# Logarithms of both parities of w in two steps, an earlier output of step 7, and halved dummy matmuls in an attention-then-MoE kernel

## The chip, the cores and the metric

The kernel runs on one core of a Trainium2 chip. The metric is the device time of one execution in microseconds (us), lower is better; where several executions were timed, the median is given. A core has five engines with a queue each: TensorE (PE in the profile, its weight loads PEld), VectorE (DVE), ScalarE (ACT), GpSimd (POOL) and SyncE (SP, which here issues all DMAs). Each engine does its instructions in the order of its queue, and waits on semaphores for the others.

## The reference

A recurrence over 768 positions (4 batches, 8 heads, 48 channels a head), whose output goes through two matrices with a squared ReLU between them:

```python
for t in range(S):
    cur = einsum('bhd,bhe->bhde', u[None] * k[t], v[t])
    y[t] = einsum('bhd,bhde->bhe', r[t], state + cur)
    state = w[t][:, :, :, None] * state + einsum('bhd,bhe->bhde', k[t], v[t])
x = y.transpose(0, 2, 1, 3).reshape(3072, 384)
out = maximum(x @ w_in, 0) ** 2 @ w_out        # w_in 384 x 2048, w_out 2048 x 384
```

All inputs and the output are float32; the values of w lie between 0.8 and 0.95.

## The kernel before

The 3072 tokens are done in 12 steps of 256. A tile has 128 partitions, and partition p holds two successive tokens, the *parities* j = 0 and 1. So `raw["w", s]` is `[128, 8 heads, 2 parities, 48]`.

**The attention half of a step** turns the recurrence into matmuls over chunks of 128 tokens. `ww_` multiplies the w of both parities (line 272), `lw_` takes the logarithm of the product on ScalarE (276) into `lw_buf`, and `cum_` sums the logarithms along the chunk with two triangular matrices, `tri_strict` and `tri_incl_neg`, and for each half chunk with `half_ones` (332 to 336) into a PSUM tile `att`. `exp_` (348) makes the decays of it in place, and `ac_` (354) those of a whole half chunk. `rd_.s.0` and `rd_.s.1` (366, 369) multiply r and k with the decays on VectorE. In the first steps TensorE transposes them (`tr_`, 382) and `rkt_` copies the results to SBUF (396), in later steps a DMA does (`dtr_`). `p_` (422, 425) multiplies the two, `pm_` (438, 441) masks the result, `su_` (453) makes the change of the state, `ts_` and `sn_` (463, 468) the next state, `y_` and `yc_` (490, 502) the output. The part with u goes beside this: `ku_` (305) multiplies k by u, `qp_` (310) by r, `q_` (315) sums over the channels, `qs_` and `vs_` (285) rearrange rows, `vq_` (324) multiplies. `ysb_` (513) adds it to the output into `y_sb`, and `yt_` with `xt_` (525, 530), or a DMA `dyt_` (534), transposes that to `xT`. `rw_` and `kw_` (294, 298) multiply r and k of one parity with w beforehand, `v_` (280) casts v.

**The MoE half of a step** is `m1_.s.g` (545, six 256-wide matmuls, g from 0 to 7), `rl_` (ReLU), `sq_` (square), `m2_` (576), `os_` and `store`.

**Order.** The scheduler is off. The string `ORDER` holds words, and each engine's queue is the order of its own words there. A word is an operation, the step and further numbers; `=V`, `=A`, `=G` name the engine where there is a choice (VectorE, ScalarE, GpSimd), and `:0` to `:3`, `:m`, `:b` the PSUM bank or banks. `ld.` words are loads on SP. Attention of steps 0 to 2 fills the opening; then the MoE half of a step and the attention of later steps share TensorE.

**Dummies.** `warm_.n.i.x` (596) puts n matmuls of 512 columns into bank i whose result nobody reads. They are in TensorE's queue like any other work, and stand only ahead of the first MoE matmul, `m1_.0.3`. There are 51 of them.

Of the kernel before, what the change touches and what calls it, by code (L numbers as in the profile page):

```python
# [16 lines left out]
ORDER = """  # L17
ld.0.w ld.0.k ld.0.u ld.0.r ld.1.w ww_.0=V lw_.0 warm_.11.5.0 cum_.0:0 ub_.0:2 kw_.0=G exp_.0 uc_.0=A warm_.4.5.1
rd_.0.1 ld.0.v tr_.0.1:0 rkt_.0.1=A ld.1.k ld.1.r rw_.0=G ld.2.w ku_.0=G rd_.0.0 ld.1.v warm_.3.5.2 tr_.0.0:1 ww_.1=V
rkt_.0.0=A qp_.0=V ld.2.r v_.0=A warm_.5.5.3 p_.0.0:m p_.0.1:1 ac_.0 lw_.1 q_.0 su_.0:b ld.2.k cum_.1:0 ts_.0.0=A  # L20
kw_.1=G pm_.0.0 pm_.0.1 vs_.0.0=A sn_.0.0 ld.1.i exp_.1 rw_.1=G vs_.0.1=A qs_.0=A warm_.3.2.4 ku_.1=G rd_.1.0 rd_.1.1
warm_.2.2.5 ts_.0.1=V qp_.1=V warm_.7.2.6 ld.0.i tr_.1.0:0 rkt_.1.0=V warm_.2.3.21 tr_.1.1:2 ac_.1 sn_.0.1 q_.1
ww_.2=G rkt_.1.1=A vs_.1.0=A lw_.2 v_.1=G y_.0:0 yc_.0.1 warm_.2.3.22 p_.1.1:1 p_.1.0:m warm_.6.1.7 vq_.0=G pm_.1.1
cum_.2:1 vs_.1.1=A pm_.1.0 qs_.1=A exp_.2 warm_.4.1.8 su_.1:m kw_.2=G ysb_.0=V rw_.2=G ts_.1.0=V warm_.1.0.23 y_.1:0
rd_.2.1 yc_.1.0 rd_.2.0 yt_.0:1 xt_.0=V sn_.1.0 cast.i.1=A vq_.1=G ts_.1.1=V warm_.1.0.24 tr_.2.1:2 yc_.1.1 ld.2.v
tr_.2.0:0 m1_.0.3:1 rkt_.2.1=A m1_.0.2:2 ac_.2 ysb_.1=V yt_.1:3 rkt_.2.0=A sn_.1.1 p_.2.1:1 rl_.0.3=A cast.i.0=V
p_.2.0:0 xt_.1=A ku_.2=V m1_.0.1:0 vs_.2.1=G m1_.1.0:3 m1_.1.2:1 vs_.2.0=A rl_.0.1=A m1_.1.1:0 v_.2=G rl_.0.2=A
rl_.1.0=A rl_.1.2=A qp_.2=G pm_.2.1 pm_.2.0 su_.2:1 rl_.1.1=V ts_.2.0=V ld.2.i m1_.0.0:2 m1_.1.3:1 cast.i.2=A y_.2:1
q_.2 yc_.2.0 sn_.2.0 yc_.2.1 rl_.1.3=A m1_.0.5:3 ld.3.i m1_.1.5:1 ld.3.w m1_.0.4:0 rl_.0.0=A rl_.0.5=V qs_.2=A
rl_.1.5=A cast.i.3=G m1_.1.7:3 ld.0.o m1_.1.4:1 vq_.2=V ysb_.2=V rl_.0.4=A rl_.1.7=A ww_.3=G cast.o.0=G m1_.0.7:2  # L30
yt_.2:3 ld.2.o m1_.0.6:0 lw_.3 cast.o.2=G cum_.3:1 xt_.2=V rl_.0.7=V ld.3.o m1_.2.4:3 rl_.0.6=V sq_.0.1=A ld.1.o
sq_.0.0=A rl_.1.4=A m1_.2.2:2 sq_.0.2=A m1_.1.6:0 m1_.2.7:1 ld.3.r rl_.1.6=A sq_.1.1=A rl_.2.2=V rl_.2.4=V m1_.2.5:2
# [617 lines left out]
```

## Time and profile before

| | |
|---|---|
| time, median of 3 runs | 178.65 us (178.42 to 179.02) |
| the profiled execution | 178.38 us |
| its span, first to last instruction | 176.6 us |
| TensorE busy | 171.2 us, 97% of the span |
| VectorE busy | 138.4 us, 78% |
| ScalarE busy | 134.0 us, 76% |
| GpSimd busy | 110.0 us, 62% |

A row of the timeline gives start, duration, engine, line, operation, output<-inputs, shapes and a count; in brackets stands how long the engine was idle before and who released it. Two rows from the beginning of GpSimd's timeline, the last of its memsets and its first product:

```profile
3.12 0.53 POOL L248 MEMSET lw_buf<- 128x512 bf16 x1
6.19 1.00 POOL L298 TENSOR_TENSOR k_raw<-k_raw,w_raw 128x384 f32<-128x384 f32 x1 [2.55 <-DMA k_raw<-in_k_dram]
```

The chain of waits that ended last lies on TensorE for 91% of the span; most of it is the MoE matmuls of lines 545 and 576, and 3.7% are dummies of line 596.

### The profile page before, as it was taken

The page shows a single profiled execution, that of the slowest core. Times are in us where ns is not written, and L with a number is a line of the kernel's source. Part 1 is how long each engine was busy: PE and PEld are TensorE (multiplying, and loading weights), DVE is VectorE, ACT ScalarE, POOL GpSimd, SP SyncE. Part 2 cuts the span into 40 slices and gives each one's busy share as a digit, 9 for nine tenths or more (in the row PEclk, how much of TensorE's full clock was granted, in tenths as well). Part 3 has the DMA queues.
Part 4 walks back from the last instruction along what each step waited for, and adds up shares of the span by engine and source line. Part 5 has one row for each costly group of instructions (what it writes and reads, how often), then busy time and mean ns, then how long its engine had stood idle before and what let it go on. Part 6 is the DMA issues. An engine that isn't in the chain of part 4 may idle for free.

```text
span 176.6 us, 5525 instructions
## 1 busy us (share of the span) xinstructions
PE 171.2 (97%) x2296; PEld 124.7 (71%) x2296; DVE 138.4 (78%) x205; ACT 134.0 (76%) x240; POOL 110.0 (62%) x132
## 2 busy tenths in 40 slices
PE   7889999999999999999999999999999999999993
PEld 2355488887766777678677777688776778768763
DVE  5499999779997998998988989976779693804430
ACT  5497999999899659899889979779976428863501
POOL 6558999860796147998599788979997803000000
PEclk9999999999999999999999999999999999999999
DMA  5999999999999599999999999997956710622203
GB/s 140 262 261 265 304 352 344 366 346 253 262 261 284 123 147 234 183 282 256 276 266 159 234 234 234 186 198 163 298 138 126 105 29 17 106 59 89 89 4 134
DMA packets 78954, 35.61 MB, mean 202 GB/s; under 512 B 72145, under 2 KB 77394, under 8 KB 78930
## 3 DMA queue, kind: packets, MB, share of 16 engines
q1 hardware_dynamic: 78930, 35.27, 89.2%
q8 instruction: 18, 0.29, 0.7%
q14 instruction: 6, 0.05, 0.1%
HBM read 25.17 MB, written 4.72 MB: 169 GB/s over the span
## 4 chain that ended last, share of the span: by engine, by line
PE 91%; DVE 3%; DMA 2%; ACT 1%; issue 1%; DVEq 0%; ACTq 0%
PE m L545 19%; PE m L576 18%; PE bk L576 18%; PE bk L545 17%; PE att L490 3%; DMA w_raw<-in_w_dram 2%; PE m L596 2%; PE att L502 2%; PE att L453 2%; PE att L425 2%; PE bk L596 2%; DVE ww L272 1%; PE att L334 1%; PE bk L382 1%; PE att L332 1%
## 5 line engine op out<-in xcount | busy, mean ns | idle before, releaser
L545 PEld LDWEIGHTS <-wi_sb 128*128 128x128 bf16 x576 | 54.8, 98 | 10.0 <-DMA xT<-y_sb 0.2
L576 PEld LDWEIGHTS <-gt 128*128 128x128 bf16 x400 | 37.7, 98 | 19.5 <-ACT gt L562 0.2
L545 PE MATMUL m<-xT,wi_sb 128*128 128x256 bf16 x300 | 39.4, 273 | 0.0
L562 ACT ACTIVATE gt<-gt 128x1024 bf16<-128x1024 f16 x37 | 38.2, 1052 | 0.5
L545 PE MATMUL bk<-xT,wi_sb 128*128 128x256 bf16 x276 | 36.5, 273 | 0.0
L576 PE MATMUL bk<-wo_sb,gt 128*128 128x384 bf16 (+2 forms) x208 | 36.0, 314 | 0.0
L576 PE MATMUL m<-wo_sb,gt 128*128 128x384 bf16 x192 | 35.0, 326 | 0.0
L554 ACT ACTIVATE gt<-m 128x512 f16<-128x512 f32 x32 | 18.8, 595 | 11.0 <-PE m L545 10.6
L554 ACT ACTIVATE gt<-bk 128x512 f16<-128x512 f32 x36 | 21.0, 596 | 7.6 <-PE bk L545 7.4
L556 DVE TENSOR_SCALAR gt<-m 128x512 f16<-128x512 f32 x18 | 12.3, 687 | 13.0 <-PE m L545 12.6
L441 DVE TENSOR_TENSOR pmT<-att,mask 128x1024 bf16<-128x1024 f32 x16 | 19.1, 1215 | 1.1 <-PE att L425 0.9
L324 POOL TENSOR_TENSOR ku<-v_sh,qs 128x768 f32<-128x768 bf16 x9 | 13.3, 1475 | 8.6 <-ACT qs L285 8.5
L468 POOL TENSOR_TENSOR S<-t_state,ac_buf 128x192 bf16<-128x192 f32 x20 | 11.9, 595 | 10.0 <-DVE t_state L463 9.0
L305 POOL TENSOR_TENSOR ku<-k_raw,u_bc 128x768 f32<-128x768 f32 x9 | 16.7, 1855 | 0.6 <-DMA k_raw<-in_k_dram 0.6
L298 POOL TENSOR_TENSOR k_raw<-k_raw,w_raw 128x384 f32<-128x384 f32 x8 | 8.0, 1005 | 9.9 <-DMA k_raw<-in_k_dram 9.9
L513 DVE TENSOR_TENSOR y_sb<-att,ku 128x768 bf16<-128x768 f32 x12 | 11.5, 954 | 3.5 <-PE att L490 1.5
L369 DVE TENSOR_TENSOR kdec_buf<-k_raw,att 128x768 bf16<-128x768 f32 x12 | 11.4, 947 | 3.1 <-ACT att L348 3.1
L285 ACT CAST v_sh<-v_raw 64x384 bf16<-64x384 f32 x26 | 13.2, 509 | 0.3
L310 POOL TENSOR_TENSOR ku<-ku,r_raw 128x768 f32<-128x768 f32 x7 | 12.7, 1809 | 0.2
L366 DVE TENSOR_TENSOR rdec_buf<-r_raw,att 128x384 bf16<-128x384 f32 x24 | 12.2, 544 | 0.4 <-POOL r_raw L294 0.4
L285 POOL CAST v_sh<-v_raw 64x384 bf16<-64x384 f32 x18 | 10.6, 589 | 1.4 <-DMA v_raw<-in_v_dram 0.5
L315 DVE TENSOR_REDUCE q<-ku 128x16 f32<-128x768 f32 x12 | 11.3, 944 | 0.1
(107 smaller groups left out, 255.0 us busy)
## 6 DMA issues: line engine op xcount, KB each, us to landing
w_raw<-in_w_dram SPq DMA_DIRECT2D x12, 384.0 KB, 5.6
k_raw<-in_k_dram SPq DMA_DIRECT2D x12, 384.0 KB, 6.4
r_raw<-in_r_dram SPq DMA_DIRECT2D x12, 384.0 KB, 5.7
v_raw<-in_v_dram SPq DMA_DIRECT2D x12, 384.0 KB, 6.2
out_dram<-o_sb SPq DMA_DIRECT2D x23, 192.0 KB, 3.3
w_st<-in_moe_w_in_dram SPq DMA_DIRECT2D x4, 768.0 KB, 8.9
w_st<-in_moe_w_out_dram SPq DMA_DIRECT2D x4, 768.0 KB, 7.3
kT<-kdec_buf SPq DMA_TRANSPOSE x8, 4.6
```

The source lines that it names most:

```text
L285: copy(out[j * Q:(j + 1) * Q, c], src[c * Q:(c + 1) * Q, :, j])
L305: tensor_mul("ku_", s, h)(tiles["ku", s][:, hs], raw["k", s][:, hs, 1:3, :], u_bc[:, hs, None, :].to_broadcast([C, n, 2, D]))
L310: tensor_mul("qp_", s, h)(ku, ku, raw["r", s][:, heads(h), 0:2, :])
L324: tensor_mul("vq_", s)(vq[:], tiles["vs", s][:], tiles["qs", s][:, :, :, None].to_broadcast([C, 2, H, D]))
L366: nc.vector.tensor_mul(rdec[0][:, ps, j, :, 0:D], x[:, :, j, :].rearrange("p (a e) d -> p a e d", e=2), dec.rearrange("p (a e) d -> p a e ...
L441: nc.vector.tensor_mul(pmT, ps_p[:].rearrange("p e (x t) -> p (e x) t", t=C), mk.to_broadcast([C, 8, C]))
L468: nc.gpsimd.tensor_mul(t[:], tiles.pop(("ts", s, c))[:].rearrange("p (a d) -> p a d", a=HP), tiles["a_c", s][:, :, c, None].to_broadcast([ ...
L545: nc.tensor.matmul(ps1[:, j, :], wi_sb[:, n // 4, kk, n % 4 * 128:(n % 4 + 1) * 128], tiles["xT", s][:, :, kk, :], start=(kk == 0), stop=( ...
L554: nc.scalar.activation(rl, m1, AF.Relu, scale=RS)
L556: nc.vector.tensor_scalar(out=rl, in0=m1, scalar1=RS, scalar2=0.0, op0=ALU.mult, op1=ALU.max)
L562: nc.scalar.activation(gt, rl, AF.Square)
L576: nc.tensor.matmul(m2, gt[:, 4 * q + n, rows * C:(rows + 1) * C], wo_sb[:, 4 * q + n, cols], start=(summed[s, c] == 1 and n == 0), stop=(s ...
```

## The change

1. In steps 1 and 2 the word `ww_` is gone: `lw_` takes the logarithm of both parities at once, straight from the loaded w, into a new tile `lw_pair`, which GpSimd clears at the start. `cum_` then does each of its sums as two accumulating matmuls, one a parity.
2. `ku_.0` goes from GpSimd to VectorE, `vs_.1.0` from ScalarE to GpSimd, `rl_.6.5` from VectorE to ScalarE.
3. Some words move: in step 0 and 1 `ac_.0`, `exp_.1`, `rd_.1.1`, `qs_.1` and `su_.1`; three dummies go ahead of `tr_.0.1`, four halves ahead of `p_.0`; `m1_.3.3` goes ahead of two `m2_`; in steps 7 and 8 `vq_.7` and `ysb_.7` go ahead of `q_.8`, `ld.10.w` ahead of two transposes on SP, and `kw_.8`, `pm_.7.1`, `qs_.8`, `ww_.10` change places.
4. Dummies whose last number is 6 or more become twice as many of 256 columns: 23 of the 51 become 46. Between `p_.1.0` and `cum_.2` now stand 14 halves, then 2 ahead of `su_.1` and 8 between `su_.1` and `y_.1`; before it was 6 wholes, then 4, then 1 there.

```diff
+    SHORT = 6
+    PAIR_LN = {int(w.split(".")[1]) for w in ORDER.split() if w.startswith("lw_.")} - {
+        int(w.partition("=")[0].split(".")[1]) for w in ORDER.split() if w.startswith("ww_.")}
+    lw_pair = consts.tile([C, 2, H, DP], BF16)
...
+        if PAIR_LN:
+            nc.gpsimd.memset(lw_pair[:], 0.0)
...
     def lw_(s, h=None):
+        if s in PAIR_LN:
+            nc.scalar.activation(lw_pair[:, :, :, 0:D].rearrange("p j h d -> p h j d"), raw["w", s][:], AF.Ln)
+            return
...
     def cum_(s, h=None):
-        lw, hs = lw_bufs[s % NLW], heads(h)
+        hs = heads(h)
...
+        logs = [lw_pair[:, j] for j in range(2)] if s in PAIR_LN else [lw_bufs[s % NLW][:]]
+        ends = dict(start=(True, False), stop=(False, True)) if s in PAIR_LN else dict(start=(True,), stop=(True,))
+        sums = [(cs[:, 0, 0:n], tri_strict)] + ([] if s in ONE_SUM else [(cs[:, 1, 0:n], tri_incl_neg)])
         for p in pairs(h):
-            nc.tensor.matmul(cs[:, 0, DM + 2 * p:DM + 2 * p + 2], lw[:, 2 * p:2 * p + 2, :],
-                             half_ones[:], start=True, stop=True)
-        nc.tensor.matmul(cs[:, 0, 0:n], tri_strict[:], lw[:, hs, 0:D], start=True, stop=True)
-        if s not in ONE_SUM:
-            nc.tensor.matmul(cs[:, 1, 0:n], tri_incl_neg[:], lw[:, hs, 0:D], start=True, stop=True)
+            for lw, start, stop in zip(logs, ends["start"], ends["stop"]):
+                nc.tensor.matmul(cs[:, 0, DM + 2 * p:DM + 2 * p + 2], lw[:, 2 * p:2 * p + 2, :],
+                                 half_ones[:], start=start, stop=stop)
+        for into, tri in sums:
+            for lw, start, stop in zip(logs, ends["start"], ends["stop"]):
+                nc.tensor.matmul(into, tri[:], lw[:, hs, 0:D], start=start, stop=stop)
...
     def warm_(n, i, x=0):
-        for _ in range(n):
-            nc.tensor.matmul(quad[i][:] if i < 4 else att[i - 4][:, 0, :], warm[:, 0:C], warm[:],
-                             start=True, stop=True)
+        bank = quad[i][:] if i < 4 else att[i - 4][:, 0, :]
+        m = 512 if x < SHORT else 256
+        for _ in range(n * 512 // m):
+            nc.tensor.matmul(bank[:, 0:m], warm[:, 0:C], warm[:, 0:m], start=True, stop=True)
...
-rkt_.0.0=A qp_.0=V ld.2.r v_.0=A warm_.5.5.3 p_.0.0:m p_.0.1:1 ac_.0 lw_.1 q_.0 su_.0:b ld.2.k cum_.1:0 ts_.0.0=A
+rkt_.0.0=A qp_.0=V ld.2.r v_.0=A warm_.2.3.21 warm_.5.5.3 p_.0.0:m p_.0.1:1 lw_.1 q_.0 su_.0:b ld.2.k cum_.1:0
```

How the queues stand at three places. VectorE, from the products of r in step 0 to those of step 1, before:

```order
L366 TENSOR_TENSOR rdec_buf_109<-r_raw,att_86 128x4x2x48 x2
L272 TENSOR_TENSOR ww<-w_raw 128x384
L310 TENSOR_TENSOR ku<-ku,r_raw 128x768
L315 TENSOR_REDUCE q<-ku 128x16
L438 TENSOR_TENSOR pmT<-m_0_90,mask 128x512
L438 TENSOR_TENSOR pmT<-m_1_91,mask 128x512
L441 TENSOR_TENSOR pmT<-att_87,mask 128x1024
L366 TENSOR_TENSOR rdec_buf_111<-r_raw,att_86 128x4x2x48 x2
L369 TENSOR_TENSOR kdec_buf_112<-k_raw,att_86 128x16x48
```

and with the change:

```order
L379 TENSOR_TENSOR rdec_buf_110<-r_raw,att_86 128x4x2x48 x2
L315 TENSOR_TENSOR ku<-k_raw,u_bc 128x768
L320 TENSOR_TENSOR ku<-ku,r_raw 128x768
L325 TENSOR_REDUCE q<-ku 128x16
L451 TENSOR_TENSOR pmT<-m_0_90,mask 128x512
L451 TENSOR_TENSOR pmT<-m_1_91,mask 128x512
L454 TENSOR_TENSOR pmT<-att_87,mask 128x1024
L382 TENSOR_TENSOR kdec_buf_113<-k_raw,att_86 128x16x48
L379 TENSOR_TENSOR rdec_buf_112<-r_raw,att_86 128x4x2x48 x2
```

`ww_.1` has given its place to `ku_.0`, and the products of k in step 1 (`kdec_buf`) now come ahead of those of r (`rdec_buf`). ScalarE, from the copies of step 0 to the exponential of step 1, before:

```order
L396 COPY kT<-bk_88 128x1024
L396 COPY rT<-bk_89 128x1024
L280 CAST v_bf<-v_raw 128x8x2x48
L354 ACTIVATE ac_buf_105<-att_86 128x8
L276 ACTIVATE lw_buf_104<-ww 128x8x48
L461 COPY t_state<-bk_88 128x192
L285 CAST v_sh<-v_raw 64x384 x2
L348 ACTIVATE att_86<-att_86 128x2x384
```

and with the change:

```order
L409 COPY kT<-bk_88 128x1024
L367 ACTIVATE ac_buf_106<-att_86 128x8
L409 COPY rT<-bk_89 128x1024
L290 CAST v_bf<-v_raw 128x8x2x48
L283 ACTIVATE lw_pair<-w_raw 128x8x2x48
L474 COPY t_state<-bk_88 128x192
L361 ACTIVATE att_86<-att_86 128x2x384
L295 CAST v_sh<-v_raw 64x384 x4
```

`ac_.0` has moved up between the copies, the logarithm is twice as large, and the exponential of step 1 no longer has two casts in front of it. GpSimd, in the stretch ahead of `vq_.0`, before:

```order
L305 TENSOR_TENSOR ku<-k_raw,u_bc 128x768
L468 TENSOR_TENSOR S<-t_state,ac_buf_105 128x192
L272 TENSOR_TENSOR ww<-w_raw 128x384
L280 CAST v_bf<-v_raw 128x8x2x48
L324 TENSOR_TENSOR ku<-v_sh,qs 128x768
```

and with the change:

```order
L315 TENSOR_TENSOR ku<-k_raw,u_bc 128x768
L481 TENSOR_TENSOR S<-t_state,ac_buf_106 128x192
L295 CAST v_sh<-v_raw 64x384 x2
L290 CAST v_bf<-v_raw 128x8x2x48
L334 TENSOR_TENSOR ku<-v_sh,qs 128x768
```

The two casts of `vs_.1.0` stand where `ww_.2` stood.

More of the change, by code (lines that the diff above doesn't have):

```diff
@@ L23 @@
[L23 to L32, printed above, removed]
@@ L89 @@
+store.11.2 os_.11.3=A store.11.3
 """
```

127 lines of the change are left out of this document (68 added, 59 removed).

## The prediction

> **What bounds the kernel now.** I read the page's first line, then the busy time by stretch, then the four engines' rows of the opening in order of time.
>
> ```profile
> span 176.6 us, 5525 instructions
> 13.00:25.00 12.00, 11.69 (x174) 7.01 (x174) 12.00 (x19) 10.29 (x23) 11.32 (x12) 1.00 1.13 297
> 25.00:174.00 149.00, 148.81 (x2025) 112.68 (x2022) 117.70 (x171) 115.58 (x204) 91.38 (x104) 1.00 0.88 195
> ```
>
> The columns are stretch, length, then the busy time of PE, PEld, DVE, ACT and POOL. From 25 us on TensorE has no gap to speak of (148.81 of 149.00), and no dummy is left there. Whatever the change does after 25 us can win at most those 0.19 us. So the time is set by when the first matmul of the MoE half, `m1_.0.3`, starts: before it TensorE is kept full with dummies, and VectorE has no pause either (12.00 of 12.00). What each waits for, VectorE first:
>
> ```profile
> 9.12 1.68 DVE L272 TENSOR_TENSOR ww<-w_raw 128x384 f32<-128x384 f32 x1
> 10.72 0.94 DVE L310 TENSOR_TENSOR ku<-ku,r_raw 128x768 f32<-128x768 f32 x1
> ...
> 14.90 1.01 DVE L366 TENSOR_TENSOR rdec_buf<-r_raw,att 128x384 bf16<-128x384 f32 x2
> 15.82 0.95 DVE L369 TENSOR_TENSOR kdec_buf<-k_raw,att 128x768 bf16<-128x768 f32 x1
> ...
> 19.28 1.21 DVE L441 TENSOR_TENSOR pmT<-att,mask 128x1024 bf16<-128x1024 f32 x1
> ...
> 21.61 0.95 DVE L513 TENSOR_TENSOR y_sb<-att,ku 128x768 bf16<-128x768 f32 x1
> ...
> 24.59 0.55 DVE L530 COPY xT<-bk 128x768 bf16<-128x768 bf16 x1
> ```
>
> The last of these rows, `xt_.0`, ends at 25.14, and `m1_.0.3` starts at 25.19: VectorE's full queue is what the MoE half now waits for. TensorE over the same time:
>
> ```profile
> 7.17 1.04 PE L596 MATMUL att<-warm 128*128 128x512 bf16 x4
> 8.33 0.62 PE L382 MATMUL bk<-ident,kdec_buf 128*128 128x128 bf16 x8
> ...
> 12.37 0.25 PE L332 MATMUL att<-half_ones,lw_buf 128*128 128x2 bf16 x4
> 12.48 0.32 PE L334 MATMUL att<-lw_buf,tri_strict 128*128 128x384 bf16 x1
> 12.64 0.32 PE L336 MATMUL att<-lw_buf,tri_incl_neg 128*128 128x384 bf16 x1
> 13.31 2.75 PE L596 MATMUL m<-warm 128*128 128x512 bf16 x12 [0.34 <-DVE pmT L438]
> 15.89 0.63 PE L382 MATMUL bk<-ident,rdec_buf 128*128 128x128 bf16 x8
> ...
> 16.83 0.62 PE L382 MATMUL m<-ident,kdec_buf 128*128 128x128 bf16 x8
> 18.56 0.40 PE L422 MATMUL att<-rT,kT 64*128 64x128 bf16 x8
> 19.12 1.47 PE L596 MATMUL bk<-warm 128*128 128x512 bf16 x6
> ...
> 21.93 0.44 PE L453 MATMUL m<-v_bf,kdec_buf 64*64 64x48 bf16 x32
> 22.30 0.39 PE L596 MATMUL bk<-warm 128*128 128x512 bf16 x1
> 22.61 0.56 PE L490 MATMUL att<-v_sh,pmT 128*128 128x48 bf16 x16
> 25.19 0.82 PE L545 MATMUL bk<-xT,wi_sb 128*128 128x256 bf16 x6
> 25.84 0.82 PE L545 MATMUL m<-xT,wi_sb 128*128 128x256 bf16 x6
> ```
>
> A row's duration holds the tail of its last matmul, so I count from start to start: 12 dummies from 13.31 to 15.89, 0.215 us each.
>
> **The change, part by part.** *VectorE loses `ww_.1` and gets `ku_.0`.* `ww_.1` took 1.68 us; it ran while GpSimd did `ku_.0` (first row below, to 10.39). The new `ku_.0` has 768 elements a lane of two SBUF tensors, as the 0.94 us row at 10.72 has; the group of its own shape is slower, mean 1.05.
>
> ```profile
> 8.58 1.81 POOL L305 TENSOR_TENSOR ku<-k_raw,u_bc 128x768 f32<-128x768 f32 x1
> 12.21 1.01 POOL L298 TENSOR_TENSOR k_raw<-k_raw,w_raw 128x384 f32<-128x384 f32 x1 [1.82 <-DMA k_raw<-in_k_dram]
> 18.24 1.00 POOL L272 TENSOR_TENSOR ww<-w_raw 128x384 f32<-128x384 f32 x1
> 19.96 1.48 POOL L324 TENSOR_TENSOR ku<-v_sh,qs 128x768 f32<-128x768 bf16 x1
> L285 POOL CAST v_sh<-v_raw x4: 500/684/1142, 26.1 to 46.1; 64x384 bf16<-64x384 f32 x4
> L305 DVE TENSOR_TENSOR ku<-k_raw,u_bc 128x768 f32<-128x768 f32 x3 | 3.1, 1049 | 0.0
> ```
>
> I take 0.95, since GpSimd is then empty until its 12.21 row, which waits for a DMA: VectorE gains 1.68 - 0.95 = 0.73 us (0.63 by the mean). It would be through `pm_.0.1` and ready for step 1's decay products at 14.90 - 0.73 = 14.17.
>
> *But those need `exp_.1`, and its chain on ScalarE and TensorE gets longer.*
>
> ```profile
> 8.98 1.01 ACT L396 COPY kT<-bk 128x1024 bf16<-128x1024 bf16 x1 [1.24 <-PE bk L382]
> 10.08 1.01 ACT L396 COPY rT<-bk 128x1024 bf16<-128x1024 bf16 x1
> 10.99 0.83 ACT L280 CAST v_bf<-v_raw 128x768 bf16<-128x768 f32 x1
> 11.72 0.18 ACT L354 ACTIVATE ac_buf<-att 128x8 f32<-128x8 f32 x1
> 11.79 0.52 ACT L276 ACTIVATE lw_buf<-ww 128x384 bf16<-128x384 f32 x1
> 13.52 0.79 ACT L348 ACTIVATE att<-att 128x768 f32<-128x768 f32 x1
> 17.48 1.01 ACT L396 COPY kT<-m 128x1024 bf16<-128x1024 bf16 x1 [0.44 <-PE m L382]
> ```
>
> 1. Three dummies now stand ahead of `tr_.0.1`: seven from 7.17 take 7 x 0.215 = 1.50, so it starts at 8.67, not 8.33.
> 2. On ScalarE `rkt_.0.1` moves from 8.98 to 9.32. A 1.01 us copy frees the engine after 0.91 (10.08 to 10.99); `ac_.0`, now behind it, after 0.07 (11.72 to 11.79). `rkt_.0.0` at 10.30, `v_.0` at 11.21, and after 0.73 (10.99 to 11.72) `lw_.1` at 11.94.
> 3. `lw_.1` has 768 elements instead of 384. The cast of 768 took 0.83, the exponential of 768 0.79: 0.83, with 0.52 and twice that as the far ends. It ends at 12.77 instead of 12.31.
> 4. `cum_.1` then runs 4 more two-column matmuls at (12.48 - 12.37)/4 = 0.03 and two more at 0.16 (12.48 to 12.64): +0.43 on the 0.59 from 12.37 to the end of the 12.64 row. From 12.83 to 13.85.
> 5. `exp_.1`, no longer behind two casts, runs 13.9 to 14.7, against 13.52 to 14.31. VectorE goes on at about 14.8, against 14.90.
>
> So 0.6 of the 0.73 us turns into a wait of VectorE. The ends of step 3 move this by -0.3 and +0.2.
>
> *The decay products change places.* Before, the products of r were ready at 15.91 and transposed while those of k were made; `tr_.1.1` began at 16.83. Now k comes first, but TensorE still transposes r first, and r is ready at 14.8 + 0.87 + 1.01 = 16.68. Then `tr_.1.0` goes at 16.74 and `tr_.1.1` 0.45 later (its 0.62 less the tail of 0.17 by which the 25.19 row outlasts the next start): 17.19, +0.36. `rkt_.1.1` goes from 17.48 to 17.84 and `p_.1.1` from 18.56 to 18.92. VectorE has its `pm_.1.1` ready for it at about the old 19.28, so it loses only 0.1 here.
>
> *TensorE from `p_.1.1` to `y_.1`.* Work, all in one queue: the p matmuls 0.56 (18.56 to 19.12), 14 half dummies, `cum_.2` 0.43 + 0.43 (12.37 to 12.64 and 0.16, and step 4), 2 halves, `su_.1` 0.37 (21.93 to 22.30), 8 halves. A half costs 0.109: the 25.19 and 25.84 rows are six 256-wide matmuls in 0.65, each with its weight load. That gives 0.56 + 1.53 + 0.86 + 0.22 + 0.37 + 0.87 = 4.41, and `y_.1` at 23.33 instead of 22.61. It was waiting for `y_sb`, which ended at 22.56; with VectorE 0.1 later that wait ends before the dummies do. From `y_.1` to `m1_.0.3` were 2.58 us. One dummy of 0.215 in them now stands further ahead, so at most 2.37 is left; some of that was waiting for VectorE, as `m1_.0.3` itself did, and I put it at 0.2, an estimate: 23.33 + 2.17 = 25.50. **`m1_.0.3` comes 0.3 us later**, bounded by VectorE's 0.1 below and by ScalarE above: its `rkt_.2` copies follow `tr_.2.1`, 0.4 late.
>
> *Steps with cover.* The clearing of `lw_pair` comes before GpSimd's first product, which waits for a DMA. The Ln of step 2 adds 0.3 us to ScalarE, which in the same place gives two casts of `vs_.1.0` away. Both at 0; without cover 0.3 for the Ln and 1.1 for the clearing, twice what the 0.53 us memset of half the size took.
>
> The price of a half dummy could be otherwise by one rule: the Trainium skill, "TensorE: Matmul & The Clock Gate", Back-to-back issue gap, gives a sustained stream of weight loads and matmuls about 131 ns per matmul at N=512 and 81 ns at N=128, by which two halves would cost more than a whole. Here the trace has 215 ns at 512 and 109 ns at 256, so it differs, and the rows stand; by the page the 46 halves would add at least 46 x 81 - 23 x 131 = 713 ns, an estimate.
>
> *Step 7.* `y_sb` of step 7 moves ahead of the reduction `q_.8`.
>
> ```profile
> 113.67 0.55 PEld L545 LDWEIGHTS <-wi_sb 128*128 128x128 bf16 x6 [0.25 <-DMA xT<-y_sb]
> 113.68 0.83 PE L545 MATMUL m<-xT,wi_sb 128*128 128x256 bf16 x6
> ```
>
> Its transposed copy is what the first weight load of `m1_.7.7` waited 0.25 us for. TensorE itself shows no gap, so I count 0 (to -0.2, the whole idle time above). `q_.8` and `qs_.8` come that much later; they feed `y_sb` of step 8, two steps of TensorE work on. `ld.10.w` passes the two transposes of step 7 in SP's queue, whose results `p_.7` takes; this, `m1_.3.3`, `kw_.8` and `rl_.6.5` on ScalarE lie where TensorE shows no wait: 0, and at most a few tenths if one of them makes a wait.
>
> **Sum.** The profiled execution took 178.38 us (span 176.6 and 1.8 around it): 178.38 + 0.3 = 178.68. The median of the three runs is 0.27 above that execution, so the forecast is 178.65 + 0.3 = **178.95**, itself between 178.5 and 179.4. About 0.3%, here 0.54 us, is what a measurement of this kernel can tell from no change.
>
> **Rivals.** *Faster: VectorE's gain goes through.* VectorE is the engine without a pause; if `exp_.1` ends by 14.1, so an `lw_.1` 0.6 us earlier than I work out, `p_.1.1` comes at 18.92 - 0.63 = 18.29. TensorE's 4.41 us then bring `y_.1` to 22.70 and `m1_.0.3` to 24.9, 0.3 early: 178.35. The whole 0.7 (177.95) would also need dummies shorter than their rows. For it: VectorE's full row. Against: steps 1 to 4, each from a row. Chance 0.18, of which I give a third to more than 0.54 us.
>
> *Slower: GpSimd becomes the bound of `y_sb`.* `ww_.2` (18.24, 1.00) is replaced by the two casts of `vs_.1.0`, at 0.50 to 1.14 each. At 1.14 each `vq_.0`, which ended at 21.44, ends at about 22.7; VectorE's `ysb_.0` starts 1.1 late, and everything behind it in VectorE's full queue to `xt_.0`: 178.65 + 1.1 = 179.75. At 0.50 each nothing changes; it decides from about 1.4 us for both. In that slot the three GpSimd rows of before show no slowing, so I hold it for the less likely end, 0.20. The Trainium skill, "GPSIMD Engine Reference", Specifications, says the SBUF interfaces are shared with VectorE, in contention with instructions of two SBUF inputs. The 1.68 us `ww_.1` beside GpSimd agrees; VectorE's work in the new slot has mostly a PSUM input, so the rule speaks for the low end.
>
> *Nothing in the opening moves the end*: the dummies only fill what is waited for, 178.65. Chance 0.10; the forecast has 0.52.
>
> **How the numbers follow.** Faster by over 0.54 us (under 178.11) is a third of the first rival, 0.06, and 0.06 for causes that I don't see: 0.12. Slower (over 179.19) is the second rival and the upper part of the forecast, 0.10: 0.30. The rest, 0.58, is within. The range runs from 178.1, which takes in the first rival's likely price, to 179.7, which takes in most of the second's.
>
> **What would show it.** Right: VectorE idle about 0.6 us before the products of k of step 1, released by `exp_.1`; `tr_.1.1` near 17.2; no TensorE wait between the 14 halves and `y_.1`; `m1_.0.3` near 25.5; the rest without gaps. Wrong: `exp_.1` ending before 14.2; `vq_.0` ending after 21.7; halves not at 0.109; or TensorE gaps after 26 us.

## The result and the profile after

| | before | changed |
|---|---|---|
| median of 7 runs, us | 178.49 | 180.21 |
| lowest to highest | 178.42 to 179.02 | 179.48 to 181.62 |
| profiled execution, its span | 178.38, 176.6 | 179.86, 178.1 |

The changed kernel takes 1.0096 of the time of before, 95% interval 1.0076 to 1.0117: it is slower by 1.4 to 2.1 us. The forecast, 178.95 with a range up to 179.7, was too fast. The runs of the changed kernel also lie further apart than those of before, 2.1 us against 0.6.

First the opening. These are TensorE's rows of the changed kernel in order of time (start, duration, engine and line, what is written and read, and in brackets the wait ahead of a row), then two of ScalarE and one of VectorE:

```profile
16.75 0.56 PE L395 MATMUL bk<-ident,rdec_buf 128*128 128x128 bf16 x7 [0.23 <-DVE rdec_buf L379]
17.14 0.61 PE L395 MATMUL m<-ident,kdec_buf 128*128 128x128 bf16 x8
...
19.01 0.40 PE L435 MATMUL att<-rT,kT 64*128 64x128 bf16 x8
...
19.57 1.70 PE L611 MATMUL bk<-warm 128*128 128x256 bf16 x14
21.11 0.34 PE L346 MATMUL att<-half_ones,lw_pair 128*128 128x2 bf16 x8
...
22.64 1.05 PE L611 MATMUL bk<-warm 128*128 128x256 bf16 x8
23.53 0.56 PE L503 MATMUL att<-v_sh,pmT 128*128 128x48 bf16 x16
...
25.77 0.82 PE L558 MATMUL bk<-xT,wi_sb 128*128 128x256 bf16 x6
```

```profile
11.88 0.86 ACT L283 ACTIVATE lw_pair<-w_raw 128x768 bf16<-128x768 f32 x1
...
13.92 0.80 ACT L361 ACTIVATE att<-att 128x768 f32<-128x768 f32 x1 [0.97 <-PE att L350]
```

```profile
14.81 0.95 DVE L382 TENSOR_TENSOR kdec_buf<-k_raw,att 128x768 bf16<-128x768 f32 x1 [0.44 <-POOL r_raw L304]
```

The order of events is the forecast one, row by row, and the first matmul of the MoE half, `m1_.0.3`, starts at 25.77 instead of 25.19: 0.58 us late. VectorE's bracket names GpSimd as the releaser; the exponential that it also needs ended at 14.72.

This lag gets smaller by itself at 85 us. Same two places of TensorE's queue, before and then changed (the transposes of the output of step 6, and eight matmuls behind the products of step 6):

```profile
83.28 0.50 PE L525 MATMUL bk<-ident,y_sb 128*128 128x128 bf16 x6
...
85.33 1.47 PE L576 MATMUL bk<-wo_sb,gt 128*128 128x384 bf16 x8
```

```profile
83.87 0.50 PE L538 MATMUL bk<-ident,y_sb 128*128 128x128 bf16 x6
...
85.64 1.47 PE L589 MATMUL bk<-wo_sb,gt 128*128 128x384 bf16 x8
```

It is 83.87 - 83.28 = 0.59 ahead of the products and 85.64 - 85.33 = 0.31 behind them; before lost 0.28 us within rows that count as busy, and the changed kernel did not.

Then comes step 7. TensorE's queue around the first matmul of step 7's MLP, `m1_.7.7`, before and changed:

```profile
109.75 4.06 PE L576 MATMUL bk<-wo_sb,gt 128*128 128x384 bf16 x24
113.68 0.83 PE L545 MATMUL m<-xT,wi_sb 128*128 128x256 bf16 x6
```

```profile
110.07 4.06 PE L589 MATMUL bk<-wo_sb,gt 128*128 128x384 bf16 x24
115.15 0.83 PE L558 MATMUL m<-xT,wi_sb 128*128 128x256 bf16 x6 [1.02 <-DMA xT<-y_sb]
```

Ahead of the 24 matmuls the lag is 0.32 us; behind them it is 115.15 - 113.68 = 1.47. TensorE ran out of work and waited for the transposed output of step 7, `xT`, which a DMA brings. In TensorE's list of waits from 20 to 175 us that is the only entry of the changed kernel, where before has none:

```profile
PE m L558 <- DMA xT<-y_sb: 1.0, 1, 1.0
```

And 1.47 is the whole difference of the two executions, 179.86 - 178.38 = 1.48. So in them the lag of the opening accounts for 0.3, and what was lost at the wait, 1.47 - 0.32 = 1.15, for the rest.

The DMA was issued sooner than before, since VectorE's sum `ysb_.7` comes sooner, but it took longer. VectorE and SP's queue in the changed kernel, then SP's queue of before:

```profile
105.96 1.69 DVE L334 TENSOR_TENSOR ku<-v_sh,qs 128x768 f32<-128x768 bf16 x1
107.75 0.96 DVE L526 TENSOR_TENSOR y_sb<-att,ku 128x768 bf16<-128x768 f32 x1
```

```profile
107.16 0.53 SPq L183 DMA_DIRECT2D k_raw<-in_k_dram  x1
108.74 1.28 SPq L547 DMA_TRANSPOSE xT<-y_sb  x1
```

```profile
106.62 0.53 SPq L179 DMA_DIRECT2D k_raw<-in_k_dram  x1
109.31 1.22 SPq L534 DMA_TRANSPOSE xT<-y_sb  x1
```

From its issue at 108.74 to TensorE at 115.15 it took 6.4 us; before, from 109.31 to 113.68, 4.4 us. Of the 2.0 us more, 0.57 are only the sooner issue: the DMA still stands behind the loads of v of step 9 and k of step 10, and the load of k was itself issued 0.54 later than in before (107.16 against 106.62). In the trace the first packet of the transposing DMA leaves at 111.17, before at 110.66, so 0.51 later. The other 0.96 were lost in the transfer itself, from its first packet to the start of `m1_.7.7`: 3.98 us against 3.02. What the DMA engines did meanwhile is in the row of GB/s, 40 slices of 110.5 to 115 us, so 0.1125 us each, before and changed:

```profile
GB/s 256 293 215 225 369 228 132 16 9 7 9 7 14 16 23 9 11 9 9 16 266 271 329 324 328 259 208 287 266 263 266 270 270 253 356 259 259 328 396 323
```

```profile
GB/s 270 266 259 249 259 265 297 237 246 248 396 36 11 7 9 7 9 7 9 200 272 273 307 147 0 0 0 0 7 7 9 9 10 10 10 10 253 266 55 242
```

Before, all queues stand almost still once, for 13 slices (1.5 us, from 111.3). In the changed kernel they do so twice, for 7 slices (0.8 us) from 111.85 and, after half a microsecond of traffic, for 12 slices (1.35 us) from 113.2.

### The profile page after: what moved, and what is told of

It reads as the page before. It is cut to its first block, busy times and chain, and to the rows that moved or that the text cites. A ratio compares the mean times of both kernels' runs of the same rounds, so it can differ in the third digit from the quotient of the medians.

```text
span 178.1 us, 5594 instructions
## 1 busy us (share of the span) xinstructions
PE 172.2 (97%) x2329; PEld 127.8 (72%) x2331; DVE 137.9 (77%) x204; ACT 133.8 (75%) x239; POOL 109.3 (61%) x133
## 3 DMA queue, kind: packets, MB, share of 16 engines
HBM read 25.17 MB, written 4.72 MB: 168 GB/s over the span
## 4 chain that ended last, share of the span: by engine, by line
PE 82%; DMA 7%; DVE 4%; SPq 3%; POOL 1%; issue 1%; ACT 0%; DVEq 0%; POOLq 0%
PE m L558 18%; PE m L589 18%; PE bk L558 17%; PE bk L589 14%; DMA xT<-y_sb 4%; DMA k_raw<-in_k_dram 3%; PE att L503 3%; SPq L183 2%; PE att L515 2%; PE att L466 2%; PE bk L611 2%; PE att L438 1%; PE att L350 1%; PE bk L395 1%; DVE ku L334 1%; DVE pmT L451 1%
## 5 line engine op out<-in xcount | busy, mean ns | idle before, releaser
L567 ACT ACTIVATE gt<-m 128x512 f16<-128x512 f32 x33 | 19.3, 593 | 11.5 <-PE m L558 11.4
L569 DVE TENSOR_SCALAR gt<-m 128x512 f16<-128x512 f32 x17 | 11.6, 687 | 13.1 <-PE m L558 12.5
L315 POOL TENSOR_TENSOR ku<-k_raw,u_bc 128x768 f32<-128x768 f32 x8 | 15.2, 1900 | 1.1 <-DMA k_raw<-in_k_dram 1.1
L308 POOL TENSOR_TENSOR k_raw<-k_raw,w_raw 128x384 f32<-128x384 f32 x8 | 8.6, 1077 | 10.6 <-DMA k_raw<-in_k_dram 10.6
L295 POOL CAST v_sh<-v_raw 64x384 bf16<-64x384 f32 x20 | 12.4, 622 | 1.7 <-DMA v_raw<-in_v_dram 0.8
L295 ACT CAST v_sh<-v_raw 64x384 bf16<-64x384 f32 x24 | 12.2, 508 | 1.0 <-DMA v_raw<-in_v_dram 0.7
L611 PEld LDWEIGHTS <-warm 128*128 128x128 bf16 x74 | 7.3, 104 | 6.6 <-issue 3.0
```

The source lines that it names most:

```text
L295: copy(out[j * Q:(j + 1) * Q, c], src[c * Q:(c + 1) * Q, :, j])
L315: tensor_mul("ku_", s, h)(tiles["ku", s][:, hs], raw["k", s][:, hs, 1:3, :], u_bc[:, hs, None, :].to_broadcast([C, n, 2, D]))
L567: nc.scalar.activation(rl, m1, AF.Relu, scale=RS)
L569: nc.vector.tensor_scalar(out=rl, in0=m1, scalar1=RS, scalar2=0.0, op0=ALU.mult, op1=ALU.max)
```

## The experiments

All times stand beside runs of before on the same chip, whose medians were 178.19 to 178.27. "MLP" is the start of `m1_.0.3`, "wait" TensorE's wait for `xT` of step 7; both are of the profiled execution, whose time stands beside them.

| kernel | median (lowest to highest, runs) | ratio to before, 95% | MLP | wait | profiled |
|---|---|---|---|---|---|
| e1_opening | 179.69 (179.13 to 180.82, 6) | 1.0052 to 1.0095 | 26.20 | 1.31 | 180.82 |
| e2_step7 | 178.22 (178.11 to 180.07, 12) | 0.9989 to 1.0033 | 25.30 | 1.45 | 180.07 |
| e3_ldw | 178.20 (177.94 to 179.54, 12) | 0.9988 to 1.0020 | 25.08 | 0 | 178.39 |
| e4_step7_noldw | 178.17 (177.88 to 178.83, 12) | 0.9981 to 1.0007 | 25.17 | 0.22 | 178.83 |
| g1_halves | 178.25 (177.84 to 179.34, 12) | 0.9989 to 1.0023 | 25.14 | 0 | 178.37 |
| g2_lag | 178.93 (178.70 to 179.29, 11) | 1.0024 to 1.0046 | 25.96 | 0 | 179.03 |
| g3_whole | 179.56 (178.52 to 180.32, 11) | 1.0035 to 1.0078 | 25.64 | 0 | 178.52 |
| g4_fewer | 179.41 (178.47 to 181.16, 12) | 1.0039 to 1.0085 | 25.45 | 0 | 178.62 |
| h1_pair | 179.39 (179.08 to 179.69, 6) | 1.0052 to 1.0083 | 25.65 | 0.61 | 179.68 |
| h5_cover | 180.14 (179.65 to 180.76, 6) | 1.0089 to 1.0127 | 25.63 | 0.23 | 180.76 |
| h6_cover_before | 179.55 (179.15 to 179.89, 6) | 1.0059 to 1.0091 | 25.08 | 0 | 179.15 |
| h7_fewer_cover | 179.54 (179.37 to 180.10, 6) | 1.0061 to 1.0096 | 25.99 | 0 | 180.04 |
| k1_k10_behind | 179.16 (178.60 to 179.48, 6) | 1.0032 to 1.0061 | 26.27 | 0 | 179.15 |
| k2_k10_before | 178.44 (178.16 to 179.43, 12) | 1.0002 to 1.0030 | 25.14 | 0 | 178.57 |
| k3_lag12 | 179.13 (178.60 to 179.81, 12) | 1.0031 to 1.0064 | 25.63 | 0.36 | 179.07 |
| k4_pair_less | 179.71 (179.13 to 180.04, 6) | 1.0058 to 1.0089 | 25.72 | 1.01 | 179.76 |
| l1_after_again | 179.75 (178.56 to 180.99, 10) | 1.0056 to 1.0104 | 25.79 | 1.47 | 180.99 |
| l2_better | 178.53 (178.28 to 178.87, 12) | 1.0001 to 1.0021 | 25.30 | 0 | 178.58 |

From the start of `m1_.7.7` to the end of the span every one of these profiled executions takes 62.8 to 63.1 us, before and the changed kernel 62.9. So whatever a profiled execution loses against before, it has lost by then.

### Which part of the change

The first suspect was the new order of step 7, since the wait stands there. *e1_opening*: the code and the words of the changed kernel up to the output of step 6, the words of before behind it.

```diff
-dtr_.7.0 exp_.8 sn_.7.0 ts_.7.1=V kw_.8=V ... pm_.7.1 pm_.7.0 vq_.7=V ... y_.7 ysb_.7=V ... ww_.10=G rl_.6.5=A q_.8
+dtr_.7.0 exp_.8 kw_.8=V sn_.7.0 ts_.7.1=V ... pm_.7.0 pm_.7.1 ... y_.7 ... q_.8 qs_.8=G ww_.10=G rl_.6.5=V vq_.7=V ... ysb_.7=V
```

> The change up to the output of step 6 as it is, steps 7 and 8 in the order of before. Theory A (two losses: the opening starts the MLP 0.3 to 0.6 us later, and the new order of step 7 makes TensorE wait about 1 us for the transposed output of step 7): TensorE's first multiplication of step 0's MLP starts near 25.8 us as in the changed kernel, its 20 to 174 us show no wait for xT of step 7 above 0.3 us, and the time is 0.2 to 0.6 us over before (178.7 to 179.1). Theory B (the order of step 7 does nothing; the later start alone moves the transposing DMA into other traffic): the wait of about 1 us is here too and the time is that of the changed kernel, 1.5 to 1.7 us over before. Theory C (the opening costs nothing at the end, since the work after it absorbs it): within 0.2 us of before.

*e2_step7*: the reverse, before with only the new words behind the output of step 6.

> The kernel of before with the new order of steps 7 and 8 alone, the opening untouched. Theory A: TensorE waits 0.8 to 1.5 us for the transposed output of step 7, and the time is 0.8 to 1.3 us over before (179.3 to 179.8). Theory B: no wait beyond 0.3 us, and the time is that of before within 0.2 us.

*e3_ldw* and *e4_step7_noldw* split this part once more.

```diff
-dyt_.6 dtr_.7.1 dtr_.7.0 exp_.8 ... ld.9.r ld.10.w sn_.7.1
+dyt_.6 ld.10.w dtr_.7.1 dtr_.7.0 exp_.8 ... ld.9.r sn_.7.1
```

> The kernel of before with one word moved: the load of w of step 10 ahead of the two transposes of step 7 on SP. Theory A1 (this load, now ahead of the transposes, shifts every DMA behind it by half a microsecond and is what step 7 loses by): 0.6 to 1.2 us over before, with the wait for xT of step 7. Theory A2 (what costs is the order of the products of v, of the sum and of the transpose itself, i.e. that the transpose is issued closer behind the load of k of step 10): within 0.3 us of before, no wait above 0.4 us.

> The kernel of before with the new order of steps 7 and 8, but with the load of w of step 10 left behind the load of r of step 9, where it was. Theory A1 (that load is the cause): within 0.3 us of before, the transpose of step 7 takes some 4.3 us and TensorE waits no more than 0.3 us for it. Theory A2 (the order of step 7 itself is the cause): 0.8 to 1.3 us over before, the transpose takes about 6 us, as in the run with all of the new order.

The suspicion fell: the opening alone costs 0.5 to 0.95%, nearly all of the loss, and has the wait at step 7 although that step is ordered as before; the new order of step 7 alone costs nothing that can be measured, and neither do its two parts, the earlier load of w (*e3*) and the rest without it (*e4*, with a wait of 0.22 in its profile). The profile of e2_step7 is still worth a look, since the profiled execution was, at 180.07, the slowest of the twelve, of which the median was 178.22:

```profile
115.38 0.83 PE L545 MATMUL m<-xT,wi_sb 128*128 128x256 bf16 x6 [1.45 <-DMA xT<-y_sb]
```

So the wait of step 7 exists there too, and by the times of the other runs in few executions. It looks like an event that comes or does not come, and that the opening brings in most of them. Each kernel left one profile, so how often it comes is read from the times and was not seen.

### The lag or the number of instructions

*g1_halves*: before with only its dummies cut in halves, from the fourth group on.

```diff
+    SHORT = 3
...
+        m = 512 if x < SHORT else 256
+        for _ in range(n * 512 // m):
+            nc.tensor.matmul(bank[:, 0:m], warm[:, 0:C], warm[:, 0:m], start=True, stop=True)
```

> The kernel of before, with nothing changed but its dummies: from the third group on (the words that end in 5.3 and later) each is cut into two of half the width, so the same dummy time in 33 multiplications more, that is 66 more instructions of TensorE (the changed kernel has 35 multiplications more). It leaves no work out. Theory L (being later is what makes the wait for xT of step 7: the opening's lag of 0.5 us meets the transposing DMA): no lag, no wait, within 0.2 us of before. Theory I (more TensorE instructions ahead of step 7 move TensorE's instruction fetches, which go through the same DMA engines, onto that transposing DMA, which stands still meanwhile): a wait of 0.5 to 1.5 us for xT of step 7 and a time 0.5 to 1.5 us over before, without a lag in the opening. Rival of my prediction's answer on the halves (they cost 0): the opening itself later by more than 0.2 us.

*g2_lag*: before with three whole dummies ahead of `m1_.0.3`.

```diff
+warm_.3.1.30 m1_.0.3:1
```

> The kernel of before with three whole dummies (0.645 us at 215 ns each) put right ahead of TensorE's first multiplication of step 0's MLP, 3 multiplications more in all. Theory L: that start goes from 25.2 to about 25.8, the lag stands at 0.5 to 0.65 us until step 7, there TensorE waits another 0.5 to 1.5 us for the transposed output, and the time is 1.2 to 1.9 us over before, like the opening of the change. Theory I: the lag alone, 0.5 to 0.7 us over before, and a wait at step 7 of at most 0.3 us. Theory C (the lag is absorbed): within 0.2 us of before.

*g3_whole*: the changed kernel with whole dummies (`SHORT = 99`). *g4_fewer*: the changed kernel without `warm_.1.0.24` and `warm_.4.1.8`.

> The changed kernel with all its dummies whole (23 multiplications fewer, the same dummy time); the rest of the change stays. Theory L: as the changed kernel, 1.3 to 1.8 us over before, with the wait for xT of step 7. Theory I: the opening's lag of 0.5 us stays and the wait at step 7 gets smaller or goes: 0.4 to 0.9 us over before.

> The changed kernel without the two dummy groups that stand around the state update of step 1 (ten halves, 1.09 us of TensorE); no work of the reference is left out. If TensorE's own work between the second products of step 1 and its output sets the start of the MLP (my prediction's count), that start goes from 25.77 to about 25.4, where VectorE's copy of the transposed output of step 0 (24.84 to 25.39 in the changed kernel) takes over as the bound, and the time falls by 0.3 us or more against the changed kernel; with theory L by up to 0.8, since a smaller lag also shortens the wait at step 7. If VectorE's chain alone sets it, nothing moves: within 0.2 us of the changed kernel.

Halves alone cost nothing: 1.0006 with an interval of 0.9989 to 1.0023. A lag alone costs itself and no more: 178.93 - 178.20 = 0.73 us in the medians for 0.645 us of dummies, all eleven runs under 179.3, no wait at step 7. Both theories that name one of the two alone have fallen. And neither dummies nor halves alone are what makes the changed kernel slow: without the halves, or without the ten around `su_.1`, it is still 0.35% or more over before, and its runs still spread over 1.8 us and, leaving out the slowest of g4_fewer, 2.2 us (178.47 to 180.64). Whether they add some tenths is not resolved, since these intervals overlap with that of the changed kernel. The start of the MLP in g4_fewer moved to 25.45 as worked out, so TensorE's queue of dummies did set it in the changed kernel; but their profiled executions (178.52 and 178.62) were among their fastest, without the wait, and the medians are 0.8 to 1.0 us above them.

### The pairs, and a cover for the wait

*h1_pair*: before without the words `ww_.1=V` and `ww_.2=G`, so the logarithms of steps 1 and 2 are taken of both parities at once, all else in its old place, dummies whole.

> The kernel of before with only the logarithms of steps 1 and 2 taken of both parities at once (the two products ww of these steps fall out, the sums of logarithms are read twice); no word is moved and the dummies stay whole. VectorE gets 1.68 us free at 11.5, but the sums of step 1 take 0.43 us more, the logarithm 0.3 us more. Theory P (the part of the change that makes step 7 wait is this one): 0.8 us or more over before, or a spread of its runs of over 1.5 us, with a wait for xT of step 7. Theory O (it is the new order and the moved work of the opening): within 0.4 us of before and its runs within 1 us of each other. If the free time of VectorE goes through, the MLP starts before 25.0 and the time falls by up to 0.7 us; by my prediction it does not, since the exponentials of step 1 come late.

*h5_cover* (on the changed kernel) and *h6_cover_before* (on before) put other work in TensorE's queue where the wait was:

```diff
-m1_.7.7:2 ... os_.6.0=V m2_.6.1.2 os_.6.1=A
+m2_.6.1.1 m2_.6.1.2 m1_.7.7:2 ... os_.6.0=V os_.6.1=A
```

> The changed kernel with two groups of the second multiplication of step 6 (4 multiplications each, 0.67 us) moved ahead of TensorE's first multiplication of step 7's MLP, so that this multiplication needs its transposed input 1.35 us later; nothing else is changed. Theory S (what the change loses at the end, beyond the opening's lag of 0.3 us, is the wait for xT of step 7): no or a short wait there, 178.4 to 178.9, and a spread of the runs under 1 us. Theory N (the loss lies elsewhere, or another transposed output becomes late in its place): still 179.3 or more, with the wait at another place.

> The kernel of before with the same two groups moved ahead of step 7's MLP. Theory S: before has no wait there to hide, so within 0.2 us of before; the tail of its runs (up to 178.97 and 179.25) gets shorter. If the move costs something by itself (steps 8 and 9 of the attention come 1.35 us later on TensorE), it shows here, and is to be taken off the run of the changed kernel with the same move.

*h7_fewer_cover*: h5 without the two dummy groups and with whole dummies.

> A try at a better version: the changed kernel with the same two groups moved, without the two dummy groups around the state update of step 1, and with whole dummies. The MLP starts near 25.4 instead of 25.77 and the wait at step 7 is covered. Theory S: 178.2 to 178.6, level with before and some 1.5 us under the changed kernel. Theory N: 179 or more.

The pairs alone cost 0.5 to 0.8%, with `m1_.0.3` at 25.65 and the wait at step 7. VectorE's 1.68 us do not come through, in large part because with `ku_.0` still on GpSimd VectorE waits for that instead:

```profile
10.38 0.96 DVE L320 TENSOR_TENSOR ku<-ku,r_raw 128x768 f32<-128x768 f32 x1 [1.21 <-POOL ku L315]
```

The covers are a miss in one way: the move itself costs before 1.3 us in the medians, so no version with it is good. In the profile of h6_cover_before TensorE waits 0.48 us for ScalarE's `gt` and 0.28 for `o_sb` near 119 us, where before has neither; together they are about the 0.77 by which that execution is over the one of before, and what the slower runs lose beyond it is not known. h5_cover still has 0.23 us of the wait. But the two together answer the question: with the same cover on both, the changed kernel is 180.14 - 179.55 = 0.59 us over before, instead of 1.5 to 1.7. What is left is about its lag at the start of the MLP, 25.63 - 25.08 = 0.55, though that the two are one thing is argued from their size. h7 is level with h6 in the median, though 178.2 to 178.6 was expected of it if the wait was the whole loss, and its profiled execution enters the MLP at 25.99; it agrees, but proves little.

### The queue ahead of the transposing DMA

*k1_k10_behind* (changed kernel) and *k2_k10_before* (before) issue that DMA ahead of a load:

```diff
-ld.10.k dyt_.7 v_.9=A
+dyt_.7 ld.10.k v_.9=A
```

> The changed kernel with the load of k of step 10 issued behind the transposing DMA of step 7's output instead of ahead of it. Theory Q (the wait for xT of step 7 is time in the queue: that DMA's packets go only after the loads of v of step 9 and k of step 10, 1.4 us each): the transposed output lands 1.0 to 1.5 us sooner, TensorE does not wait there, and the time is 0.3 to 0.7 us over before with a spread under 1 us. Rival: the DMA stands still in the same way wherever it is in the queue, or k of step 10 is then late for GpSimd: 1.2 us or more over before.

> The same move in the kernel of before, as the control: no wait is there to remove, so theory Q gives no change (within 0.2 us). If the late load of k of step 10 costs something, it shows here and is to be taken off the run of the changed kernel.

*k3_lag12* gives before the lag in as many matmuls as the pairs add; *k4_pair_less* the pairs with three dummies fewer.

```diff
+        m = 512 if x < 30 else 128
...
+warm_.12.1.30 m1_.0.3:1
```

> The kernel of before with twelve narrow dummies (128 columns) ahead of TensorE's first multiplication of step 0's MLP: about 0.65 us of lag in 12 multiplications, as many as the paired logarithms add. Theory T (lag and number of TensorE instructions together bring the wait at step 7): 0.9 to 1.5 us over before, as with the pairs alone, with a wait for xT of step 7. Theory R (it is something else in the pairs: the work taken from VectorE and GpSimd, the w buffers that are read later): 0.6 to 0.8 us over before, no wait beyond 0.3 us, a spread under 0.8 us.

> The kernel of before with the paired logarithms of steps 1 and 2 and three whole dummies fewer between the sums of step 2 and the state update of step 1 (0.645 us), no word moved. The start of the MLP comes back to 25.1 to 25.3. If the lag is all that the pairs cost (with whatever wait it brings at step 7): within 0.3 us of before. If the wait at step 7 comes with the pairs whether they lag or not (theory R): still 0.5 us or more over before, with that wait in its profile.

One load moved takes 0.6 to 1.0 us off the changed kernel (179.16 against 179.75 and 180.21, the medians of its two series), while it costs before 0.02 to 0.30%. The medians come from different chips, but the interval of k1_k10_behind, 1.0032 to 1.0061, lies below that of the changed kernel, 1.0076 to 1.0117, and overlaps only a little with that of its second series, 1.0056 to 1.0104. Its profile has no wait left at step 7: the DMA landed at 113.88, 0.6 us ahead of TensorE. Its profiled execution is 179.15 - 178.38 = 0.77 us over before, which is the lag with which it enters the MLP, 26.27 - 25.19 = 1.08, less what comes back at 85 us; at step 7 it is 114.47 - 113.68 = 0.79:

```profile
26.27 0.82 PE L558 MATMUL bk<-xT,wi_sb 128*128 128x256 bf16 x6
...
114.47 0.82 PE L558 MATMUL m<-xT,wi_sb 128*128 128x256 bf16 x6
```

k3_lag12 suggests that the lag and the number of TensorE instructions work together: its twelve runs fall apart into five at 178.60 to 178.69, which by their times have the lag alone, and seven at 179.07 to 179.81; the profile, of one at 179.07, has a wait of 0.36 at step 7. Three matmuls with the same added time (0.65 against 0.67 us) had given a narrower spread, up to 179.29. But those two ran on different chips, so this is not shown.

k4_pair_less did not do what it was for: the start of the MLP stayed at 25.72, so it does not part the pairs from their lag. Why it stayed is in its profile: VectorE now pauses ahead of the product of k of step 2, for the exponentials that ScalarE makes late, behind a logarithm of 0.84 instead of 0.53. The bracket names no releaser ("issue"); that the product waits for the exponentials is read from the rows, which end at 23.23 where it starts at 23.32.

```profile
19.80 0.84 ACT L283 ACTIVATE lw_pair<-w_raw 128x768 bf16<-128x768 f32 x1
...
22.44 0.79 ACT L361 ACTIVATE att<-att 128x768 f32<-128x768 f32 x1
```

```profile
23.32 0.96 DVE L382 TENSOR_TENSOR kdec_buf<-k_raw,att 128x768 bf16<-128x768 f32 x1 [0.55 <-issue]
```

### The changed kernel once more, and a try at a better one

> The changed kernel once more, unchanged. If its loss is an opening lag of 0.5 to 1.0 us and a wait of 0 to 1.5 us for xT of step 7 that differs from execution to execution: a median of 179.5 to 180.3, 1.3 to 2.0 us over before, runs spread over 1.5 us or more, and the profiled execution's time over before is its lag at the MLP's start plus its wait at step 7, within 0.2 us.

The second series of the changed kernel gives 1.0056 to 1.0104 and runs from 178.56 to 180.99: its fastest run is about as far over before as the lag alone would have it, its slowest 2.4 us above that. Its profiled execution is that slowest, and there the DMA took 116.29 - 109.2 = 7.1 us:

```profile
116.29 0.83 PE L558 MATMUL m<-xT,wi_sb 128*128 128x256 bf16 x6 [1.47 <-DMA xT<-y_sb]
```

The lag (0.60) and the wait (1.47) make 2.07 of its 2.6 us over the profiled execution of before; the sum that the expectation asked for misses by 0.5, of which 0.3 is another wait in that execution, of `m1` for ScalarE's `gt`.

*l2_better* takes the 0.73 us from VectorE without the pairs:

```diff
-ku_.0=G rd_.0.0 ... ww_.1=V ... vs_.0.0=A sn_.0.0 ld.1.i exp_.1 ... rd_.1.0 rd_.1.1 ... warm_.7.2.6
+ww_.1=G rd_.0.0 ku_.0=V ... exp_.1 vs_.0.0=A sn_.0.0 ld.1.i ... rd_.1.1 rd_.1.0 ... warm_.4.2.6
-tr_.1.0:0 rkt_.1.0=V warm_.2.3.21 tr_.1.1:2 ... rkt_.1.1=A
+tr_.1.1:2 rkt_.1.1=V warm_.2.3.21 tr_.1.0:0 ... rkt_.1.0=A
```

> The kernel of before with the product ww of step 1 on GpSimd in place of the product ku of step 0, which goes to VectorE (1.68 us there against 0.95: 0.73 us less, as in the change), the exponentials of step 1 ahead of the copies of v on ScalarE, k ahead of r in step 1 (products and transposes), and three dummies fewer ahead of the first of these transposes. No pairs, the order from step 2 on as before. If VectorE sets the MLP's start, as the prediction read it, it goes from 25.2 to 24.5 to 24.7 and the time falls to 177.5 to 177.9 (0.3 to 0.7 us under before). If ScalarE, GpSimd or a load takes over as the bound, the start stays above 25.0 and the time is within 0.2 us of before. If the earlier work meets the transposing DMA of step 7 badly, a wait for xT of step 7 eats the gain: 178.0 to 179.0.

It is no better: 1.0001 to 1.0021, the MLP at 25.30, and it ended 0.29 us over before, where within 0.2 was expected. VectorE did not get its 0.73 us. The product `ku_.0` took 1.35 us beside GpSimd's `ww_.1`, not 0.95, and its queue started 0.36 us late in this execution:

```profile
7.68 0.95 DVE L369 TENSOR_TENSOR kdec_buf<-k_raw,att 128x768 bf16<-128x768 f32 x1 [2.67 <-ACT att L348]
...
9.48 1.35 DVE L305 TENSOR_TENSOR ku<-k_raw,u_bc 128x768 f32<-128x768 f32 x1
```

No version here beats before.

## Why the prediction was wrong, step by step

- **VectorE's gain turns into a wait.** Right. The exponentials of step 1 were put at 13.9 to 14.7 and ran 13.92 to 14.72; VectorE went on at 14.81 (14.8). It stood 0.44 us, not 0.6: the gain of 0.73 was taken from the durations of two rows, while from start to start of the products it is (10.72 - 9.12) - (10.09 - 9.11) = 0.62.
- **The decay products and their transposes.** Right: `tr_.1.1` at 17.14 (17.19), `p_.1.1` at 19.01 (18.92).
- **TensorE from `p_.1.1` to `y_.1`.** Right in its mechanism: 23.53 - 19.01 = 4.52 us, worked out at 4.41, without a wait between. A half dummy is (21.11 - 19.57)/14 = 0.110 us, as taken from the rows; and g1_halves found no cost of 33 more matmuls. The Trainium skill, "TensorE: Matmul & The Clock Gate", Back-to-back issue gap, gives the sustained figures per matmul from which the prediction worked out 0.7 us for the halves, as an estimate. No run here bears that estimate out, and the measurement stands.
- **The start of the MLP.** A size too small: 0.58 us instead of 0.31; the 0.27 more are the 0.09, 0.11 and 0.07 by which `p_.1.1`, the queue to `y_.1` and the stretch from there to `m1_.0.3` (2.24 against 2.17) each came out longer. g2_lag shows that such a lag reaches the end. By itself this term would have given 178.65 + 0.58 = 179.2, within the range.
- **The rival with GpSimd.** Did not happen: its product for `ysb_.0` ended at 21.52, where 21.7 was the mark.
- **Step 7 at 0.** This is the step that failed: "TensorE itself shows no gap, so I count 0", and of the moved steps "at most a few tenths if one of them makes a wait". The row with the wait of 0.25 us was quoted and read as a chance to win 0.2. It says more: in that execution TensorE reached `m1_.7.7` at the moment at which its input landed, so nothing was left between the two, and every delay of that DMA beyond TensorE's own is a delay of the kernel. It was shown to be this: the wait is in the profiles of the changed kernel (1.02 and 1.47 us), of its opening alone and of the pairs alone; it goes when the DMA stands one load earlier in its queue, and 0.6 to 1.0 of the 1.5 to 1.7 us go with it. A TensorE gap after 26 us was among the prediction's own signs of being wrong, and it is the one that came.
- **Which part brings the wait** was wrong in my first reading of the result too: not the new order of step 7, which by the times alone brings it in few runs, but the opening, and of it the pairs, some 90 us ahead.
- **"At most 0.19 us after 25 us"** was not the bound it was taken for: the changed kernel got 0.28 us of its lag back at 85 us, within rows that count as busy, which a list of idle times does not show. And I used it as if it bounded the loss too.

What stays open is why the opening brings the wait in most executions. Count the runs that are slower than the lag alone explains: with a lag of 0.645 us in three matmuls there are none, with a lag in twelve 7 of 12, with 33 matmuls and no lag hardly any, with the pairs and their lag all six. These counts go by the times of the runs, on different chips, so a part of lag and count is suggested and not shown. A second standstill of the queues is not what the waits have in common: in the profiles of e1_opening, e2_step7, h1_pair, k4_pair_less and l1_after_again there is one between issue and landing, as in before. What nearly all have in common is SP's queue ahead of the DMA. The load of v of step 9 is issued at 105.86 or later in every profile with a wait (105.94 in the changed kernel, 106.97 in e1_opening) but e4_step7_noldw (104.79, wait 0.22), and at 105.75 or sooner in every one without (105.41 in before), but k1_k10_behind (106.07), in which one load less stands ahead of the DMA. So the lag may reach the DMA through the loads ahead of it. That is read off from where the profiles agree; no run moved this alone.

## What to carry to other kernels

A wait of a tenth or two for a transfer, with no gap behind it, was here not a small thing to win but the sign of a margin of zero: price it as the whole of what the transfer can lose, and look first whether the transfer can stand further forward in its queue; here that took back about half of the loss, and cost before itself 0.02 to 0.30%. A cost that comes and goes between runs of one kernel is read from the spread of the times, not from one profile: in e2_step7, runs of one kernel were up to 1.9 us apart, with that wait in the profile of the slowest. And 1.7 us taken from a full engine were worth nothing here, where the work that replaces them stands on the chain that this engine waits for next.
